# An attention and MLP block on one core: seven weight slices prepared during the first row maxima, later loads respaced, one pair of products left in its place

## The chip, the core and the metric

The kernel runs on one core of a Trainium2 chip. The core has TensorE (matrix products, into PSUM), VectorE, ScalarE and GpSimd (called POOL in the profile), which work in parallel, each on its own instructions and strictly in their order. SyncE (SP) issues all DMAs of this kernel, also in order: where a DMA's operand isn't ready, SP waits, and all DMAs behind it wait with it. The metric is the device time of one execution in microseconds. The kernel before took 1708.81 us (median of 3 runs, 1708.61 to 1709.07).

## What is computed

One transformer block with modulation (adaLN), sequence 2048, width 512, 32 heads of 16 columns, MLP width 1792, all in float32:

```
mod = silu(c) @ w_mod              # six vectors sa, ca, ga, sb, cb, gb
h = layernorm(x) * (1 + ca) + sa
x = x + ga * (softmax(q k^T / 4) v, all heads) @ wo       # q, k, v from h @ wqkv
h = layernorm(x) * (1 + cb) + sb
x = x + gb * mish(h @ w1 + b1) @ w2
```

## The kernel before

**Precision.** Operands of most products are split in a high and a low part (`hi_copy`, `lo_sub`, lines 89 and 97), and a product is made as high*high + high*low + low*high. Weights are split once by the kernel itself and put into scratch in DRAM: 14 slices of w1, 4 of wo, 14 of w2, each 128x512, called preps here. wo and w2 are multiplied by a gate before the split; w1 is not. `prep_unit` (line 656) loads a raw slice (256 KB), splits it on POOL five half-steps later and puts both halves back (512 KB) nine or more half-steps after the load.

**Groups and steps.** The 2048 rows are cut in 4 blocks of 512, the heads in 8 groups of four, so there are 32 groups n of 16 steps t each. A step works on two things at once. It makes scores of its own group, 128 keys by 512 queries for four heads (`score`, products on line 531), with exponentials on ScalarE into tiles `p0` to `p3` (3 or 4 buffers each), and two steps later the products with the values (`pv`, line 549). And it makes row maxima of scores for the group whose scores come 20 steps later (`max_tile`, product on line 482, maximum on VectorE on line 484). When a group's maxima are complete, they are transposed (`max_rows`, line 509), split, and put as two extra rows into the group's query tile (`qa<-mt`, line 520); scores then come out with the maximum taken off. Products that use 64 rows of the array run in pairs, one on each half.

**Hooks.** Everything else is hung on half-steps: `at(h, f)` runs `f` when the program text is at half-step h = 2t or 2t+1. A hook sets the order of instructions on each engine, not a time. "Position" is h modulo 32, that is, the place in a group. Before t = 0 there are 20 steps (h = -40 to -1) that make only maxima, two double products a step (`max_pair`, line 488, products on line 496, maxima on line 498), and fill TensorE with whole units (below). The exponentials' tiles are not in use there.

**Units.** The projections of q, k and v, then for each block of rows the output projection (wo), the up products (w1) and the down products (w2), are cut in units of 6 to 12 products. In the first 20 steps `whole_units` (line 1151) runs units as they come, with the PSUM banks `ms` and `acc` in turn; later a unit's products are paired with scores and maxima in the steps (`next_part`, line 1133). When a unit is done, its `fin` empties the bank. For a unit of keys or queries this is a copy by ScalarE to `qf` (one buffer), the split by POOL into `qh` and `ql` (two buffers each), and puts to scratch (`kscr`, `qscr`) from which `load_pair` (line 316) later reads the keys and queries of two heads into `ka` and `qa` (five buffers each). In the first 20 steps the order of units is: 12 of values, 4 of keys, 1 of queries, then keys again; the fins of the four key units fall on hooks -16, -14, -10 and -8. A weight slice of q, k and v for such units is loaded by `slice_load` and split by `slice_split` (`wh` on ScalarE, `wl` on POOL).

**The early pair.** Where a unit begins in a step, the last score of the step's own half of the array and the last maximum of the other half are issued ahead of it (in `step`, line 1230). Step 2 of a group is the one in which the last products of the group before have just ended and their sums are copied out of PSUM (`ot`, line 563).

**Places in program order.** Just before the first 20 steps SP issues the constants and the copies `ka<-ka` (line 1360). At hook -40 the next slice of query weights is loaded, at hooks -22 and -8 head pairs 2 and 3, at -3 the first values. `start_preps` (line 1327) chains the preps from hook 60: `load_at` (line 193) and `store_at` (line 188) move loads and puts out of the positions around the puts of `mt` (position 26), and a load also waits for the put of the tile that it takes. The MLP opens (`prep_step`, line 1338) when both the last query unit and the last prep are through; `first_loads` (line 800) then loads what the first block needs. Scores of group n start at hook 32n, its first maxima at 32n - 40.

Of the kernel before, what the change touches and what calls it, by code (L numbers as in the profile page):

```python
# [8 lines left out]
F32 = mybir.dt.float32  # L9
F32R = mybir.dt.float32r  # L10
# [8 lines left out]
def adaln_block(ctx: ExitStack, tc: tile.TileContext, x, wqkv, wo, w1, b1, w2, c, w_mod, out):  # L19
    nc = tc.nc  # L20
    P = 128
# [4 lines left out]
    DK = D // P  # L26
    FT = F // P
    TB = 512
# [10 lines left out]
    PRO = 16 + LEAD  # L39
    CUT1, CUT2 = (0, 1), (2, 3)  # L40
    LOV = ((1,), (), (1, 3), (1, 3))
    PREP = 4
# [46 lines left out]
    def hi_copy(eng, hi, src):  # L89
        if eng == "a":  # L90
            nc.scalar.copy(hi, src)
        elif eng == "v":
            nc.vector.tensor_copy(hi, src)
        else:
            nc.gpsimd.tensor_scalar(hi, src, 1.0, 0.0, op0=ALU.mult, op1=ALU.add)

    def lo_sub(eng, lo, src, hi):
        (nc.gpsimd if eng == "p" else nc.vector).tensor_sub(lo, src, hi.bitcast(F32))  # L98
# [93 lines left out]

    def load_at(h):

        return h if h < 60 or 2 <= h % 32 < 20 else h - h % 32 + 28 if 20 <= h % 32 <= 28 else h + -(h - 2) % 32

    def at(h, f):

        hooks.setdefault(h, []).append(f)
# [98 lines left out]
    def load_q(pp, rows=50):  # L298
        n, j = divmod(pp, 2)
        qb, g = divmod(n, G)  # L300
        h = 4 * g + 2 * j
        qt = qa[pp % NR].bitcast(F32)
        assert (0, h // 8, qb) in put_away, (pp, put_away)
        for s in range(2):
            nc.sync.dma_start(qt[64 * s:64 * s + rows, :], qscr[h + s, :rows, qb * TB:(qb + 1) * TB])

    def load_k(pp, tb=None):
        n, j = divmod(pp, 2)
        h = 4 * (n % G) + 2 * j
        kt = ka[pp % NR].bitcast(F32)  # L310
        at_ = slice(0, S) if tb is None else slice(tb * TB, (tb + 1) * TB)
        assert {(1, h // 8, i) for i in (range(NB) if tb is None else (tb,))} <= put_away, (pp, put_away)
        for s in range(2):
            nc.sync.dma_start(kt[64 * s:64 * s + 48, at_], kscr[h + s, :, at_])

    def load_pair(pp):
        load_q(pp)
        load_k(pp)
# [144 lines left out]
    ap = ctx.enter_context(tc.tile_pool(name="ap", bufs=1, reuse_waits="tile"))  # L463
# [224 lines left out]
    def load_y(qb, i):  # L688
        y = mst["p"].tile([P, D], F32, tag="y", name="y", bufs=5)
        r = 4 * qb + i  # L690
        nc.sync.dma_start(y, x[r * P:(r + 1) * P, :])
        return y
# [73 lines left out]
    NA = 7  # L766
# [3 lines left out]
    def block(qb, t0):  # L770
# [3 lines left out]
        y, w1s, w2s, wos = state[qb]  # L774
# [3 lines left out]
        def load(h, d, load_, keys):  # L778

            for j, k in enumerate(keys):  # L780
                at(h + 2 * j, lambda k=k: d.__setitem__(k, load_(k)))

        def more_w2(h, n):

            for j in range(n):
                k = mst["w2 at"]
                b, i = divmod(k, DK + FT)
                mst["w2 at"] += 1
                if b < NB - 1:
                    d, f, i = (state[b][3], load_wo, i) if i < DK else (state[b][2], load_w2, i - DK)  # L790
                    load(h + 2 * j, d, f, (i,))
                    if f is load_wo and i == DK - 1:
                        mst["wo at", b] = h + 2 * j
                elif i >= DK and i < DK + 3:
                    load(h + 2 * j, state[b][2], load_w2, (i - DK,))
                else:
                    mst["w2 at"] -= 1
                    break

        def first_loads(h):  # L800
            mst["w2 at"] = 0
            more_w2(h + 1, NA)
            load(h + 2, y, lambda i: load_y(qb, i), range(4))
            load(h + 9, w1s, load_w1, range(2))
            for i in range(4):
                mst["y at", qb, i] = h + 2 + 2 * i

# [111 lines left out]
        n = len(groups)  # L919
# [21 lines left out]
        for gi in range(2):  # L941
            f = 4 * gi + 5
# [22 lines left out]
    _, w1s, w2s, wos = state[last]  # L965
# [159 lines left out]
    cur = {"left": [], "fin": None, "part": []}  # L1125
# [48 lines left out]
    def step(t):  # L1174
        second = t % 2
        n, u = t // 16, t % 16 // 2
        tm = t + PRO
        run_hooks(2 * t)
        if t < 0:

            for i in range(2):
                if tm < 16:
                    kb, jq = divmod(2 * tm + i, 8)
                else:
                    jq, kb = tm % 16 // 2, 2 * second + i
                max_pair(tm // 16, jq, kb)
            if second and tm % 16 == 15:
                neg_max(tm // 16)
            run_hooks(2 * t + 1)
            for f in ats.pop(t, []):  # L1190
                f()
            whole_units(2 * t + 1, CREDIT)
            do_specials(2 * t + 1)
            return
        s = 0 if second else 1
        own, others = ([score(n, j, v, 2 * u + i) for i in range(2) for j in range(2)] for v in (s, 1 - s))
        if not second and 1 < t < T:
            next_part(2 * t)
        part = list(cur["part"])
        f = len(part)  # L1200
        if t >= T:
            if t == T:
                cur["tag"] = "acc"
            run_hooks(2 * t + 1)
            pv(t - 2)
            whole_units(2 * t + 1, 8)
            do_specials(2 * t + 1)
            return
        if tm < T:
            o = max(0, (8 - f) // 2)  # L1210
            mo, alone = maxima(tm // 16, tm % 16 // 2, s, o)

            mine = [x for p in zip(mo, own) for x in p] + own[len(mo):]
        else:
            o = max(0, (4 - f) // 2)
            mine = own[o:] if second else own[:4 - o]
            alone = others[4 - o:] if second else others[:o]

            m = len(mine)
            if f > m:  # L1220
                mine = [mine[(i * m) // f] if (i + 1) * m // f > i * m // f else None for i in range(f)]
        beside = part + alone

        def emit(product):
            e = product()
            if e is not None and cur.pop("want", None):
                cur["after"] = e

        mid = False
        if cur.pop("new", None) and alone and len(mine) > f:  # L1230

            emit(mine.pop())
            emit(beside.pop())
        for i in range(max(len(mine), len(beside))):
            if i == len(mine) // 2:
                run_hooks(2 * t + 1)

            if not f and tm < T and i == (2 if mst.get("norming") else 3):
                pv(t - 2)
                mid = True  # L1240
            if i < f:
                last = i + 1 == f
                if i < len(mine) and mine[i] and not last:
                    emit(mine[i])
                for m in beside[i]:
                    mm_half(m, second, cur.pop("after", None))
                if last:
                    cur["want"] = True
                    if i < len(mine):
                        emit(mine[i])  # L1250
                    if second and not cur["left"]:
                        cur["fin"](2 * t + 2)
                        cur["fin"] = None
            else:
                for x in (*mine[i:i + 1], *beside[i:i + 1]):
                    emit(x)
        if tm < T and tm % 16 == 15:
            neg_max(tm // 16)
        do_specials(2 * t + 1)
        if not mid:  # L1260
            pv(t - 2)
        for f in ats.pop(t, []):
            f()
# [59 lines left out]
    preps = [(w1scr[f], w1[:, f * P:(f + 1) * P].rearrange("(k p) m -> p k m", p=P), None) for f in range(FT)]  # L1323
    preps += [(woscr[k], wo[k * P:(k + 1) * P, :], 0) for k in range(DK)]
    preps += [(w2scr[f], w2[f * P:(f + 1) * P, :], 1) for f in range(FT)]

    def start_preps(h, i=0, turn=0, puts=()):

        if i == len(preps):
            mst["open"] = (max(puts) + 2) // 2  # L1330
            return
        three = (2, 1, NKC - 1) in put_away
        prep_unit(h, three and turn % 3 == 2, *preps[i])
        puts = (*puts, store_at(h + 9))[-3 if three else -2:]
        then = load_at(max(h + PREP, puts[0] + 1 if len(puts) > 2 - (not three) else 0))
        at(then, lambda: start_preps(then, i + 1, turn + 1 if three else 0, puts))

    def prep_step(t):
# [4 lines left out]

    for n in range(NIT):
        if n > 2:
            at(32 * (n - 2) + (15 if n % 2 == 0 else 9), lambda n=n: load_pair(2 * n))
        if n > 1:
            at(32 * (n - 1), lambda n=n: load_pair(2 * n + 1))
        if n > 0:
            at(32 * n - 11, lambda n=n: load_v(n))  # L1350
    at(-3, lambda: load_v(0))
    at(17, lambda: load_pair(4))
    for qb in range(NB - 1):
        t0 = 32 * G * (qb + 1) + 16
# [15 lines left out]
    t = T + 2  # L1370
# [32 lines left out]
```

## Time and profile before

| | |
|---|---|
| median of 3 runs | 1708.81 us |
| the profiled execution | 1705.6 us |
| its span, first to last instruction | 1703.8 us |
| TensorE busy | 1675.0 us (98%) |
| VectorE, ScalarE, POOL busy | 1437.6, 1356.9, 807.6 us |
| DMA | 240.08 MB, mean 141 GB/s |

The profile shows one execution. A row of a timeline gives the start in us from the first instruction, the duration, the engine (PE is TensorE, PEld its weight loads, DVE VectorE, ACT ScalarE; SPq is an issue of a DMA by SP), the line of the kernel, the operation, output<-input by the program's names, shapes and a count of merged instructions; in brackets stands the idle time before it and what ended it. A row of the stretches gives the stretch, its length, the busy time of PE, PEld, DVE, ACT and POOL with their counts, the granted clock, the mean busy share of the 16 DMA engines, and GB/s. Ends of products are modelled, so the starts are what is read.

### The profile page before, as it was taken

Reading aid. Unit: us, or ns where it says so; the run is one execution under the profiler, and the core shown is the slowest. Engines: PE = TensorE matmul, PEld = TensorE weight load, DVE = VectorE, ACT = ScalarE, POOL = GpSimd, SP = SyncE. Lnnn points to the kernel's source line nnn. Section 1 sums busy time; section 2 is a strip of 40 time slices with the busy share of each in tenths; the row PEclk is TensorE's granted clock in tenths of the full one; section 3 lists DMA queues with packets and bytes.
Section 4 is the critical chain, followed back from the end, with each engine's and each line's share of the span. In section 5 each row is a group of like instructions: output and inputs, shape, how many; then the busy total and the mean of one; then the engine's idle time right before and its main releaser. Section 6 shows DMA issues by size and latency. Waiting matters only on the chain.

```text
span 1703.8 us, 33660 instructions
## 1 busy us (share of the span) xinstructions
PE 1675.0 (98%) x12372; PEld 915.5 (54%) x12372; DVE 1437.6 (84%) x2368; ACT 1356.9 (80%) x2613; POOL 807.6 (47%) x829
## 2 busy tenths in 40 slices
PE   7999999999999999999999999999999999999999
PEld 5755665555445455555555455555545445554587
DVE  6888888888889888888889898888889888883377
ACT  6257777777778988888888998888878988888574
POOL 5155224665413464655423564556323654555442
PEclk9999999999999999999999999999999999999999
DMA  7777457777773342434355433424354433424261
GB/s 253 187 235 214 109 162 216 237 234 222 234 208 101 99 109 76 134 80 126 83 151 148 118 74 94 139 76 126 88 143 124 124 93 83 137 68 157 84 228 63
DMA packets 113997, 240.08 MB, mean 141 GB/s; under 512 B 24048, under 2 KB 49648, under 8 KB 107784
## 3 DMA queue, kind: packets, MB, share of 16 engines
q1 hardware_dynamic: 113832, 237.92, 48.6%
q8 instruction: 98, 1.61, 0.4%
q14 instruction: 67, 0.55, 0.1%
HBM read 179.95 MB, written 51.44 MB: 136 GB/s over the span
## 4 chain that ended last, share of the span: by engine, by line
PE 84%; DMA 5%; ACT 4%; DVE 4%; issue 1%; SPq 0%; POOL 0%; ACTq 0%; DVEq 0%; POOLq 0%
PE bk L549 26%; PE ring L531 20%; PE ring L482 18%; PE bk L135 10%; PE bk L129 4%; DVE mx L484 3%; ACT pr L534 3%; PE ring L1110 2%; PE ring L129 2%; DMA qa<-mt 1%; DMA ka<-kscr 1%; PE ring L496 1%; DMA w<-woscr 1%; ACT hb L722 1%; PE ring L843 0%
## 5 line engine op out<-in xcount | busy, mean ns | idle before, releaser
L484 DVE TENSOR_REDUCE mx<-ring 128x1 f32<-128x512 f32 x1968 | 1222.0, 681 | 159.9 <-PE ring L482 142.1
L534 ACT ACTIVATE pr<-ring 128x512 f32<-128x512 f32 x2048 | 1078.2, 602 | 217.8 <-PE bk L135 128.1
L482 PE MATMUL ring<-ka,qa 64*128 64x512 f32 x1968 | 815.7, 429 | 5.2 <-ACT pr L534 3.5
L531 PE MATMUL ring<-qa,ka 64*128 64x512 f32 x2048 | 759.2, 403 | 6.5 <-DMA qa<-mt 3.7
L549 PE MATMUL bk<-pr,vg 128*32 128x512 f32 x4096 | 545.1, 604 | 0.0
L482 PEld LDWEIGHTS ring<-ka,qa 64*128 64x128 f32 x1968 | 349.1, 184 | 321.6 <-DVE mx L484 230.2
L531 PEld LDWEIGHTS ring<-qa,ka 64*128 64x128 f32 x2048 | 373.5, 184 | 200.2 <-DVE mx L484 129.8
L135 PE MATMUL bk<-h,w 64*128 64x512 f32 (+1 forms) x1080 | 279.6, 391 | 0.1
L135 PE MATMUL bk<-w,a_h 64*128 64x512 f32 x632 | 211.6, 413 | 0.3 <-ACT pr L534 0.2
L135 PEld LDWEIGHTS bk<-h,w 64*128 64x128 f32 x1080 | 178.5, 184 | 13.0 <-ACT pr L534 4.3
L549 PEld LDWEIGHTS bk<-pr,vg 128*32 128x32 f32 x4096 | 80.8, 108 | 137.7 <-issue 126.4
L135 PE MATMUL bk<-w,a_l 64*128 64x512 f32 x316 | 124.0, 392 | 0.0
L135 PEld LDWEIGHTS bk<-w,a_h 64*128 64x128 f32 x632 | 107.5, 184 | 16.9 <-ACT pr L534 8.3
L899 POOL TENSOR_TENSOR y<-yd,y 128x512 f32<-128x512 f32 x44 | 56.8, 1292 | 90.5 <-ACT yd L898 85.3
L734 POOL TENSOR_SCALAR qq<-ee 128x512 f32<-128x512 f32 x25 | 15.5, 619 | 171.5 <-ACT ee L728 171.5
L750 POOL TENSOR_TENSOR qq<-qq,rr 128x512 f32<-128x512 f32 x42 | 54.2, 1289 | 83.8 <-ACT rr L744 83.6
L736 POOL TENSOR_TENSOR hb<-hb,ee 128x512 f32<-128x512 f32 x42 | 54.1, 1287 | 82.7 <-DVE ee L732 80.7
L135 PE MATMUL bk<-w,o_hl 64*128 64x512 f32 x288 | 79.2, 404 | 0.0
L98 POOL TENSOR_TENSOR a_l<-hb,a_h 128x512 fp32r<-128x512 f32 x53 | 72.0, 1358 | 4.4
L135 PEld LDWEIGHTS bk<-w,a_l 64*128 64x128 f32 x316 | 58.3, 184 | 4.9
L135 PE MATMUL bk<-h_h,wl 64*128 64x512 f32 x168 | 57.1, 420 | 0.0
L752 POOL TENSOR_TENSOR rr<-rr,qq 128x512 f32<-128x512 f32 x42 | 54.1, 1287 | 3.5
(189 smaller groups left out, 1841.5 us busy)
## 6 DMA issues: line engine op xcount, KB each, us to landing
ka<-kscr SPq DMA_DIRECT2D x124, 384.0 KB
w<-w2scr SPq DMA_DIRECT2D x56, 512.0 KB
w<-w1scr SPq DMA_DIRECT2D x46, 512.0 KB
vg<-vscr SPq DMA_DIRECT2D x32, 552.0 KB
qa<-qscr SPq DMA_DIRECT2D x124, 100.0 KB
kscr<-qh SPq DMA_DIRECT2D x16, 512.0 KB
qscr<-qh SPq DMA_DIRECT2D x32, 256.0 KB
hl<-in_B_w SPq DMA_DIRECT2D x28, 256.0 KB
```

The costliest lines, as they stand in the source:

```text
L98: (nc.gpsimd if eng == "p" else nc.vector).tensor_sub(lo, src, hi.bitcast(F32))
L129: nc.tensor.matmul(acc, l, r, start=start, stop=stop)
L135: i = nc.tensor.matmul(acc, l[64 * g:64 * g + 64], r[64 * g:64 * g + 64], start=start and not g, stop=bool(stop and g))
L482: nc.tensor.matmul(pm, qt[64 * s:64 * s + 64, qs * P:(qs + 1) * P], kt[64 * s:64 * s + 64, kb * TB:(kb + 1) * TB], start=True, stop=True)
L484: nc.vector.tensor_reduce(out=mxs[n][:, s, 4 * j + qs, kb:kb + 1], in_=pm, op=ALU.max, axis=AX.X)
L531: nc.tensor.matmul(p_, kt[64 * s:64 * s + 64, kc * P:(kc + 1) * P], qt[64 * s:64 * s + 64, :], start=True, stop=True)
L534: e = nc.scalar.activation(pr, p_, AF.Exp, scale=SCALE)
L549: nc.tensor.matmul(accs[n][32 * h:32 * h + 32, :], vgs[n][:, o:o + 32], pts.pop((t, h)), start=(kc == 0), stop=(kc == 15))
L736: (nc.vector if tail else nc.gpsimd).tensor_mul(hb, hb, ee)
L750: nc.gpsimd.tensor_mul(qq, qq, rr)
L752: nc.gpsimd.tensor_mul(rr, rr, qq)
L899: nc.gpsimd.tensor_add(y[i], yd, y[i])
```

## The change

Seven of the 14 slices of w1 are loaded at hooks -40, -37, ... -22, split five half-steps later on POOL and put back eight after the load, in tiles `p1` and `p3`; `start_preps` begins with the eighth. `load_at` keeps loads of slices out of positions 0 to 3 (before: 0 and 1), and a load keeps two half-steps behind the put of its tile instead of one. The even head pair of a group from 3 on is loaded at position 2 (group 6: 15 as before) instead of 15 or 9. `first_loads` (called at the MLP's opening) loads the four slices of wo at once, and no longer with them three of w2 and two of w1; these five follow at hooks 279 to 287. The early pair is left in its place in step 2 of a group.

```diff
     def load_at(h):
-        return h if h < 60 or 2 <= h % 32 < 20 else h - h % 32 + 28 if 20 <= h % 32 <= 28 else h + -(h - 2) % 32
+        return h if h < 60 or 4 <= h % 32 < 20 else h - h % 32 + 28 if 20 <= h % 32 <= 28 else h + -(h - 4) % 32
...
         def first_loads(h):
             mst["w2 at"] = 0
-            more_w2(h + 1, NA)
+            more_w2(h + 1, DK)
             load(h + 2, y, lambda i: load_y(qb, i), range(4))
-            load(h + 9, w1s, load_w1, range(2))
+            load(t0 + 7, w1s, load_w1, range(2))
+            at(t0 + 10, lambda: more_w2(t0 + 11, NA - DK))
...
-        if cur.pop("new", None) and alone and len(mine) > f:
+        if cur.pop("new", None) and alone and len(mine) > f and t % 16 != 2:
...
-    def start_preps(h, i=0, turn=0, puts=()):
+    EARLY = 7
+
+    def early_prep(i, h):
+
+        scr, src, _ = preps[i]
+        lo, hi = [ap.tile([P, TB], F32R, tag=f"p{1 + i % 2 * 2}", name="ep", bufs=4) for _ in range(2)]
+        raw = lo.bitcast(F32)
+        nc.sync.dma_start(raw.rearrange("p (k m) -> p k m", m=P), src)
+
+        def split():
+            hi_copy("p", hi, raw)
+            lo_sub("p", lo, raw, hi)
+
+        def put():
+            for v, part in enumerate((hi, lo)):
+                nc.sync.dma_start(scr[:, v, :], part.bitcast(F32))
+
+        at(h + 5, split)
+        at(h + 8, put)
+
+    for i in range(EARLY):
+        at(3 * i - 2 * PRO, lambda i=i: early_prep(i, 3 * i - 2 * PRO))
+
+    def start_preps(h, i=EARLY, turn=0, puts=()):
...
-        then = load_at(max(h + PREP, puts[0] + 1 if len(puts) > 2 - (not three) else 0))
+        then = load_at(max(h + PREP, puts[0] + 2 if len(puts) > 2 - (not three) else 0))
...
-            at(32 * (n - 2) + (15 if n % 2 == 0 else 9), lambda n=n: load_pair(2 * n))
+            at(32 * (n - 2) + (15 if n == 6 else 2), lambda n=n: load_pair(2 * n))
```

## The prediction

> **What bounds the kernel now.** I read the page's totals first, then the chain of waits, then the timelines of the engines around the places that the change touches.
>
> ```profile
> span 1703.8 us, 33660 instructions
> PE 1675.0 (98%) x12372; PEld 915.5 (54%) x12372; DVE 1437.6 (84%) x2368; ACT 1356.9 (80%) x2613; POOL 807.6 (47%) x829
> ...
> PE 84%; DMA 5%; ACT 4%; DVE 4%; issue 1%; SPq 0%; POOL 0%; ACTq 0%; DVEq 0%; POOLq 0%
> ```
>
> TensorE sets the end. A step of attention ends with the eight products of probabilities with values (line 549), so their starts count the steps. A step without any wait, in the second MLP block:
>
> ```profile
> 1095.29 1.06 PE L549 MATMUL bk<-pr,vg 128*32 128x512 f32 x8
> ...
> 1098.13 1.07 PE L549 MATMUL bk<-pr,vg 128*32 128x512 f32 x8
> ```
>
> That is 2.84 us. The number of products is fixed and the change removes none, so it can win only where steps are longer, and lose only where it makes a step wait. Four of the long steps wait for a DMA:
>
> ```profile
> 339.87 0.47 PE L531 MATMUL ring<-qa,ka 64*128 64x512 f32 x1 [1.37 <-DMA qa<-mt]
> ...
> 386.84 0.47 PE L531 MATMUL ring<-qa,ka 64*128 64x512 f32 x1 [0.87 <-DMA qa<-mt]
> ...
> 434.38 0.46 PE L531 MATMUL ring<-qa,ka 64*128 64x512 f32 x1 [1.42 <-DMA qa<-mt]
> ...
> 491.77 0.46 PE L482 MATMUL ring<-ka,qa 64*128 64x512 f32 x1 [0.68 <-DMA od<-ot]
> ```
>
> The first three, 3.66 us together, are the first scores of groups 4, 5 and 6 (step 80, 96, 112), which need the row maxima (`mt`) in their query tile. The fourth, in step 132, is put down to `od<-ot`, but a maximum reads only `qa` and `ka`: it is the load of head pair 19, asked for at hook 256 and read at 264.
>
> **Part 1: no early pair in step 2 of a group.** In the step in which the sums of the group before leave PSUM (copy `ot`), ScalarE also empties the finished unit (`hb`), and the early pair puts a score first:
>
> ```profile
> 674.27 1.06 PE L549 MATMUL bk<-pr,vg 128*32 128x512 f32 x8
> 674.67 0.68 ACT L722 ACTIVATE hb<-bk,b1c 128x512 f32<-128x512 f32 x1
> ...
> 675.72 0.60 ACT L563 COPY ot<-bk 128x512 f32<-128x512 f32 x1
> ...
> 676.18 2.10 ACT L534 ACTIVATE pr<-ring 128x512 f32<-128x512 f32 x4
> ...
> 676.87 0.50 PE L482 MATMUL ring<-ka,qa 64*128 64x512 f32 x1 [0.17 <-ACT pr L534]
> ...
> 677.21 0.39 PE L531 MATMUL ring<-qa,ka 64*128 64x512 f32 x1
> ...
> 677.54 1.06 PE L549 MATMUL bk<-pr,vg 128*32 128x512 f32 x8
> ```
>
> The step takes 677.54 - 674.27 = 3.27 us, 0.43 more than 2.84. The ring has six banks, so the seventh product of the step takes the bank of the first, here the early score, whose exponential ends at about 676.87. Without the early pair the first product is a maximum and the first score the second one; the bank waited for is then wanted by the eighth product, the last. That one starts at 676.87 instead of 677.21: 0.34 us saved. What the early pair covered is the unit's bank, free when `hb` ends at 675.35, against 675.27 for TensorE's arrival (674.27 and the 1.00 us of eight products): 0.1 us, inside the wait that remains. A unit begins in such a step at 18 hooks (h = 36, 68, 260; 324 to 548 and 772 to 964 by 32). In 13 of them the step has this pattern, as here in step 482 (3.24 us):
>
> ```profile
> 1516.17 1.06 PE L549 MATMUL bk<-pr,vg 128*32 128x512 f32 x8
> ...
> 1519.41 1.06 PE L549 MATMUL bk<-pr,vg 128*32 128x512 f32 x8
> ```
>
> Of the other five, in two (548, 804) the unit before ends in a VectorE addition and the pair covers its wait, which I cost at nothing either way; three (36, 68, 868) show no such excess. 13 x 0.34 = **-4.4 us** (ends: -6 if all 18 give it, -2 if the unit's bank wait eats half).
>
> **Part 2: respaced slices and loads.** Why `mt` was late shows on SP, which issues all DMAs in order:
>
> ```profile
> 319.39 0.50 SPq L667 DMA_DIRECT2D w1scr<-hl  x1
> 326.72 0.33 SPq L660 DMA_DIRECT2D hl<-in_A_wo  x1
> ...
> 328.35 0.38 SPq L469 DMA_DIRECT2D vg<-vscr  x1
> 328.82 2.13 SPq L264 DMA_DIRECT2D qscr<-qh  x2
> ...
> 332.20 4.74 SPq L520 DMA_DIRECT2D qa<-mt  x4
> ```
>
> SP stands still from 319.9 to 326.7, because the raw slice goes into a tile whose put was issued at 319.39. Everything behind it bunches: a put, 552 KB of values and 768 KB of queries enter the queues just ahead of `mt`, whose four issues stretch to 4.74 us. I worked out the new hooks from the recurrence in `start_preps`: with 25 slices left, loads fall at positions 28, 4, 8, 12, 16 of each 32 half-steps and puts at 5, 13, 17, 21, 2 (before: loads at 28, 2, 6, 10, 14, 18). Only the load at 16 still stands three half-steps behind its tile's put (13); before, two in each group did (14 and 18), and the second started late because of the first. So SP should be on time at 21, and the bulk drains five half-steps (7 us) before `mt` at 26. I take the three waits as gone: **-3.7 us** (ends -3.7 and 0, since put, values and queries now all sit at 21). The pair loads move to position 2, right behind the other pair's at 0, which is the more urgent and stays ahead; no wait of TensorE hangs on them. At the opening of the MLP three w2 slices and two w1 slices no longer stand ahead of pair 19: **-0.7 us** (ends -0.9 and 0). MLP weights at hooks 279 to 287 are read from 300 on. The opening itself moves from step 121 to 120 only, since the last query unit (hook 237) bounds it; the second halves of the projection still wait for hook 276, so no unit moves to fill more steps.
>
> **Part 3: seven slices among the first maxima.** These are seven loads (256 KB), seven splits on POOL, fourteen puts (256 KB each), in program order at hooks -40 to -14. What stands around them:
>
> ```profile
> 70.65 3.83 SPq L1360 DMA_DIRECT2D ka<-ka  x6
> 74.53 0.65 SPq L226 DMA_DIRECT2D wr<-in_A_wqkv  x1
> ...
> 76.65 2.43 SPq L305 DMA_DIRECT2D qa<-qscr  x2
> ...
> 81.97 0.83 SPq L268 DMA_DIRECT2D kscr<-qh  x1
> ```
>
> ```profile
> 78.90 0.62 ACT L91 CAST wh<-wr 128x512 fp32r<-128x512 f32 x1 [2.37 <-DMA wr<-in_A_wqkv]
> ...
> 79.60 1.29 POOL L98 TENSOR_TENSOR wl<-wr,wh 128x512 fp32r<-128x512 f32 x1 [26.80 <-ACT wh L91]
> 81.31 0.63 POOL L95 TENSOR_SCALAR qh<-qf 128x512 fp32r<-128x512 f32 x1 [0.42 <-ACT qf L254]
> 82.02 1.29 POOL L98 TENSOR_TENSOR ql<-qf,qh 128x512 fp32r<-128x512 f32 x1
> ...
> 91.58 0.62 POOL L95 TENSOR_SCALAR qh<-qf 128x512 fp32r<-128x512 f32 x1 [4.61 <-DMA kscr<-qh]
> ...
> 93.77 0.59 ACT L254 COPY qf<-bk 128x512 f32<-128x512 f32 x1 [4.40 <-POOL ql L98]
> ```
>
> ```profile
> 50.18 0.73 PE L496 MATMUL ring<-ka,qa 64*128 64x512 f32 x4
> ...
> 88.50 1.09 PE L129 MATMUL bk<-h_h,wh 128*128 128x512 f32 x4
> ```
>
> ```profile
> 187.23 0.45 SPq L660 DMA_DIRECT2D hl<-in_B_w  x1
> ...
> 190.31 0.62 POOL L95 TENSOR_SCALAR hl<-hl 128x512 fp32r<-128x512 f32 x1 [9.27 <-DMA hl<-in_B_w]
> 191.01 1.29 POOL L98 TENSOR_TENSOR hl<-hl 128x512 fp32r<-128x512 f32 x1
> ```
>
> TensorE reaches hook -40 at 50.18, but SP gets to that hook's DMA only at 74.53: it is 24 us behind. So POOL's idle 26.80 us are not to be had: the first early load leaves at 75.2. POOL works in order too, and all seven splits (hooks -35 to -17) come ahead of its work on the first key unit (81.31; hook -16). From there the cover is gone step by step: `qf` has one buffer, so ScalarE's copy of the second key unit waits for `ql` of the first (the 4.40 us at 93.77 is that same wait); that copy frees the bank which the fourth key unit takes, at 88.50, and TensorE stops there.
>
> The floor goes by POOL alone: load in 75.2 + 3.1 (187.23 to 190.31) = 78.3; seven splits of 1.99 (190.31 to 192.30) = 92.2; the slice's `wl` 1.3, the first unit 2.0, ScalarE's copy 0.6: 96.1, against 88.50: **+7.6**.
>
> The likelier cost has the DMAs in it. Slice 4 takes slice 0's tiles and slice 6 slice 2's, so each load waits on SP for a put to land, and the next put stands behind that load. The same stretch shows 4.4 us for a load (74.53 to 78.90) and up to 9.6 for a put (81.97 to 91.58).
>
> ```profile
> 75.00:100.00 25.00, 24.78 (x116) 15.74 (x115) 22.84 (x23) 4.60 (x9) 10.22 (x11) 1.00 1.01 280
> ```
>
> With 4.4 and, for puts half as large as that key put, 6: load 0 in at 79.6, split 81.6, put landed 87.7, load 4 and put 2 behind it, landed 94.4, load 6 in at 98.9, split 100.9, first key unit 102.9, copy 103.5: +15. By bytes: seven loads, the puts of four slices ahead of the last, two value puts (544 KB each) and the query slice are 5.3 MB, 19.0 us at the 280 GB/s of the row: last load in at 94.2, its split, the first unit and the copy 4.6: 98.8, +10. The second count lets no DMA engine idle while SP waits for a put, so I take **+13.5**, nearer to the chain; with puts of 9.6 the chain gives +22. Nothing later returns it: the steps behind are paced by TensorE.
>
> The Trainium skill ("DMA: Bandwidth & Descriptors", section Anatomy of one DMA) gives about 2 us fixed plus the bytes at 436 GB/s, an estimate of 2.6 us for each of these transfers; by it POOL's chain binds and the cost is about +7. The row says 4.4 and 9.6 there, with the DMA engines full, so I go by the row.
>
> **Sum.** -4.4 - 3.7 - 0.7 + 13.5 = +4.7 us. The profiled execution took 1705.6 us (span 1703.8 and 1.8 around it), 3.2 below the runs' median 1708.8; added to that, **1713.5 us**.
>
> **Rivals.** (a) Faster: SP reaches the early loads as TensorE does, POOL does them in its idle 26.80 us before 79.60, and part 3 costs nothing: -8.8, 1700.0. It decides if the first load leaves before about 62 us (seven splits, 14 us, and a load of 3.1 then end before 79.60). Against it: the order of SP's instructions ahead of it is untouched. (b) Only POOL's floor binds: -1.2, 1707.6. (c) The long puts of 81.97 hold for the early slices, +22, and half of parts 1 and 2 comes: +17.6, 1726.4. (d) The respacing does not do what it says: put, values and queries, all at position 21, still stand in front of `mt`: 3.7 more, 1717.2.
>
> **How the numbers follow.** A measurement of this kernel tells about 0.2% (3.4 us) from no change. Forecast 0.40, (a) 0.18, (b) 0.15, (c) 0.14, (d) 0.13. Time 1713.5. Range 1703 to 1726: it holds the forecast's own range (1710 to 1715, from 10 and 15 us), (b) and (d) and reaches to (c), leaving (a) and what lies beyond (c). Slower is (c), (d) and most of the forecast, 0.62; same is (b) and the forecast's low end, 0.18; faster 0.20.
>
> **What would show it.** First early load at about 75 us; POOL's first `qh` at 95 to 101 instead of 81.31; a wait of TensorE of 8 to 15 us at the fourth key unit, put down to ScalarE's copy; first scores of step 0 later by as much; steps 80, 96 and 112 at 2.9 us; steps like the one at 674.27 near 2.9. The forecast is wrong if the first step of attention starts no later than before, or if the 3.27 us steps stay.

## The result and the profile after

| | before | after |
|---|---|---|
| median (lowest to highest), 4 runs each | 1708.71 us (1707.56 to 1709.07) | 1728.07 us (1726.04 to 1728.47) |
| the profiled execution, its span | 1705.6, 1703.8 us | 1727.78, 1726.0 us |

The ratio is 1.0119, with a 95% interval of 1.0105 to 1.0132: the changed kernel is 19.4 us slower, where +4.7 was forecast. The totals of its profile:

```profile
span 1726.0 us, 33682 instructions
...
PE 1681.4 (97%) x12372; PEld 926.1 (54%) x12372; DVE 1439.0 (83%) x2368; ACT 1358.6 (79%) x2613; POOL 808.5 (47%) x829
```

The counts on all engines are those of before, since the same work was only moved. TensorE's busy time grew by 6.4 us, the span by 22.2; most of the loss is standing still. Where it lies is read by counting steps again: the start of the products of line 549 of each step, set against the same step of before.

| from before's execution, at the products of step | 2 | 258 | 274 | 386 | 402 | last |
|---|---|---|---|---|---|---|
| after | +18.8 | +12.3 | +19.3 | +19.6 | +23.3 | +22.2 |

So 18.8 us are lost before the first step, some 7 are won over the rest, and 10.7 are lost at two places, each a few steps behind the start of a new block of rows (steps 261, 262 and 389, 390).

**Before the first step.** The timelines of SP, POOL, ScalarE and TensorE around the first key units:

```profile
75.71 2.11 SPq L1335 DMA_DIRECT2D ep<-in_B_w  x3
...
97.46 4.55 SPq L1343 DMA_DIRECT2D w1scr<-ep  x4
102.14 0.37 SPq L268 DMA_DIRECT2D kscr<-qh  x1
```

```profile
97.75 1.26 POOL L98 TENSOR_TENSOR ep<-ep 128x512 fp32r<-128x512 f32 x1
98.98 0.62 POOL L95 TENSOR_SCALAR qh<-qf 128x512 fp32r<-128x512 f32 x1
...
108.97 0.62 POOL L95 TENSOR_SCALAR qh<-qf 128x512 fp32r<-128x512 f32 x1 [5.34 <-DMA kscr<-qh]
111.03 1.28 POOL L98 TENSOR_TENSOR ql<-qf,qh 128x512 fp32r<-128x512 f32 x1 [1.44 <-DMA kscr<-ql]
```

```profile
100.98 0.59 ACT L254 COPY qf<-bk 128x512 f32<-128x512 f32 x1 [19.66 <-POOL ql L98]
...
112.34 0.59 ACT L254 COPY qf<-bk 128x512 f32<-128x512 f32 x1 [8.10 <-POOL ql L98]
```

```profile
101.61 2.07 PE L129 MATMUL bk<-h_h,wh 128*128 128x512 f32 x4 [12.86 <-ACT qf L254]
...
114.03 0.50 PE L496 MATMUL ring<-ka,qa 64*128 64x512 f32 x2 [1.66 <-DVE mt L514]
...
115.17 0.50 PE L496 MATMUL ring<-ka,qa 64*128 64x512 f32 x2 [0.64 <-DVE mx L498]
...
121.21 0.47 PE L531 MATMUL ring<-qa,ka 64*128 64x512 f32 x1 [0.80 <-DMA qa<-mt]
```

The last early split ends POOL's run at 99.0, its first key unit follows at 98.98, ScalarE's copy of the second unit has waited 19.66 us for it, and TensorE starts the fourth key unit at 101.61 instead of 88.50: 13.1 us. The rest of the 18.5 us by which the first score is late (121.21 against 102.67) lies, on TensorE's own timeline, behind that wait: 3.1 us in the three shorter waits shown, and 2.3 us at half the clock. The stretches of the same trace show the latter:

```profile
104.00:106.00 2.00, 2.00 (x7) 0.74 (x5) 0.26 (x1) 0.25 (x1) 0.00 (x0) 0.50 1.06 393
106.00:108.00 2.00, 2.00 (x9) 1.63 (x8) 2.00 (x2) 0.00 (x0) 0.00 (x0) 0.79 1.05 407
108.00:110.00 2.00, 2.00 (x12) 1.14 (x11) 1.41 (x4) 0.00 (x0) 0.62 (x1) 1.00 1.06 398
```

The granted clock (third number from the end) is 0.50 until past 106. The first twelve products behind the wait (eight of the unit, four of the maxima) take 5.03 us (to 106.64) instead of 2.71.

What TensorE waits for first need not be what makes the first score late. POOL's third key unit is late by as much: its `ql`, at 111.03 above, stood at 92.44 in the kernel before, 18.6 us earlier. Which of the two set the loss is taken up under part 3 below. The rows of the kernel before, POOL's and the first score:

```profile
92.44 1.29 POOL L98 TENSOR_TENSOR ql<-qf,qh 128x512 fp32r<-128x512 f32 x1 [0.25 <-DMA kscr<-ql]
```

```profile
102.67 0.50 PE L531 MATMUL ring<-qa,ka 64*128 64x512 f32 x1
```

**At the block boundaries.** SP, VectorE and TensorE of the changed kernel around step 261:

```profile
871.66 0.76 SPq L305 DMA_DIRECT2D qa<-qscr  x2
872.47 0.89 SPq L314 DMA_DIRECT2D ka<-kscr  x2
874.91 0.34 SPq L673 DMA_DIRECT2D w<-w2scr  x1
877.25 0.36 SPq L904 DMA_DIRECT2D out<-y  x1
877.75 0.61 SPq L574 DMA_DIRECT2D sm<-ot  x1
```

```profile
887.71 0.25 DVE L584 RECIPROCAL rc<-sm 128x16 f32<-128x16 f32 x1 [5.85 <-DMA sm<-ot]
```

```profile
880.65 1.07 PE L549 MATMUL bk<-pr,vg 128*32 128x512 f32 x8
...
888.56 0.79 PE L531 MATMUL ring<-qa,ka 64*128 64x512 f32 x1 [5.26 <-DVE mx L484]
...
889.28 1.94 PE L549 MATMUL bk<-pr,vg 128*32 128x512 f32 x8
```

And in the kernel before, SP and VectorE at the same step:

```profile
862.22 0.61 SPq L574 DMA_DIRECT2D sm<-ot  x1
...
873.23 0.69 SPq L305 DMA_DIRECT2D qa<-qscr  x2
```

```profile
869.45 0.24 DVE L584 RECIPROCAL rc<-sm 128x16 f32<-128x16 f32 x1
```

`sm` holds the sums of the group that has just ended (8 KB), and VectorE's reciprocal reads it. Before, the even pair's load was issued 11 us behind it, and the reciprocal started without a wait. Now the pair stands ahead of it as well, beside the odd pair, weights and rows of the residual that stood there before too. `sm` is issued 3.2 us later relative to the steps (15.5 us after its counterpart, where the steps are 12.3 behind), and lands 9.9 us after its issue. VectorE, in order, stops 5.85 us with the maxima behind it, and TensorE runs out of banks. The step takes 8.63 us (880.65 to 889.28).

### The profile page after: what moved, and what is told of

Read it like the earlier page. It is cut to its first block, busy times and chain, and to the rows that moved or that the text cites. A ratio compares the mean times of both kernels' runs of the same rounds, so it can differ in the third digit from the quotient of the medians.

```text
span 1726.0 us, 33682 instructions
## 1 busy us (share of the span) xinstructions
PE 1681.4 (97%) x12372; PEld 926.1 (54%) x12372; DVE 1439.0 (83%) x2368; ACT 1358.6 (79%) x2613; POOL 808.5 (47%) x829
## 4 chain that ended last, share of the span: by engine, by line
PE 87%; DMA 5%; DVE 3%; ACT 3%; SPq 1%; issue 1%; POOL 0%; ACTq 0%; POOLq 0%; DVEq 0%
PE bk L549 28%; PE ring L531 21%; PE ring L482 19%; PE bk L135 10%; PE ring L129 3%; PE ring L1111 2%; DVE mx L484 2%; ACT pr L534 2%; PE bk L129 1%; DMA sm<-ot 1%; DMA w1scr<-ep 1%; DMA kscr<-ql 1%; DMA xt<-in_A_x 1%; DMA qa<-mt 1%; DMA w<-woscr 1%
## 5 line engine op out<-in xcount | busy, mean ns | idle before, releaser
L135 PEld LDWEIGHTS bk<-w,a_h 64*128 64x128 f32 x632 | 106.9, 184 | 15.9 <-ACT pr L534 8.3
L498 DVE TENSOR_REDUCE mx<-ring 128x2 f32<-128x1024 f32 x40 | 46.8, 1218 | 19.5 <-PE ring L496 19.5
L95 POOL TENSOR_SCALAR qh<-qf 128x512 fp32r<-128x512 f32 x27 | 16.8, 621 | 88.7 <-ACT qf L254 53.6
```

What stands on the lines that cost most here:

```text
L135: i = nc.tensor.matmul(acc, l[64 * g:64 * g + 64], r[64 * g:64 * g + 64], start=start and not g, stop=bool(stop and g))
L498: nc.vector.tensor_reduce(out=mxs[n][:, :, jq, kb:kb + 1], in_=pm, op=ALU.max, axis=AX.X)
```

## The experiments

In each batch the times are set against runs of the kernel before on the same chip: 1707.72 us (17 runs) for the first four, 1708.23 us (21 runs) for the last three.

**1. The head pairs back where they were.** The changed kernel with one line undone:

```diff
-            at(32 * (n - 2) + (15 if n == 6 else 2), lambda n=n: load_pair(2 * n))
+            at(32 * (n - 2) + (15 if n % 2 == 0 else 9), lambda n=n: load_pair(2 * n))
```

> The changed kernel with the even head pairs loaded at positions 15 and 9 again, as before the change; all else as changed. Theory (pair loads): in the changed kernel two reciprocals on VectorE, in steps 261 and 389, wait 5.85 and 2.62 us for the sums (sm<-ot), whose DMA stands behind two head pairs asked for at positions 0 and 2; with the even pair back behind the sums these waits go, the steps 261, 262, 389 and 390 (8.63, 4.03, 5.11, 4.33 us) fall to about 2.9 each, and the time falls by 10.5 us from 1728.1 to about 1717.5. The waits for mt in steps 80 and 112 stay gone, since those hang on the slices. Rival (weights): the wo, w2 and y loads of the MLP at the block boundary delay the sums, and the pair is only one of several: the four steps stay above 3.5 us and the time at 1724 or more. Rival (mt): the pair at position 15 is what bunched SP in front of mt; then the waits of 1.4 us in steps 80 and 112 come back and the time is about 1721.

Measured: 1718.96 us (1717.41 to 1720.22), ratio 1.0065 [1.0052, 1.0078], 9.1 us less than after. The long steps are gone; the products of steps 260 to 262 start at

```profile
883.10 1.06 PE L549 MATMUL bk<-pr,vg 128*32 128x512 f32 x8
...
886.01 1.07 PE L549 MATMUL bk<-pr,vg 128*32 128x512 f32 x8
...
888.85 1.06 PE L549 MATMUL bk<-pr,vg 128*32 128x512 f32 x8
```

and `sm`, in SP's and VectorE's timelines, is read 7.1 us after its issue without a wait:

```profile
877.24 0.62 SPq L574 DMA_DIRECT2D sm<-ot  x1
```

```profile
884.31 0.25 DVE L584 RECIPROCAL rc<-sm 128x16 f32<-128x16 f32 x1
```

Steps 261, 262, 389 and 390 take 2.91, 2.84, 2.90 and 2.84 us, the shift stays at +14.8 to +15.2 from step 258 to 402, steps 80 and 112 stay at 2.84 and 2.85, and step 96 takes 3.57 instead of 3.25. So the pair at position 2 made the boundary stalls and had no part in the gain at `mt` of steps 80 and 112. In the profiled execution the first step starts at +20.5 instead of +18.8, so the last step is 8.1 us earlier and not 10.7.

**2. The pair rule alone.** The kernel before with the one condition:

```diff
-        if cur.pop("new", None) and alone and len(mine) > f:
+        if cur.pop("new", None) and alone and len(mine) > f and t % 16 != 2:
```

> The kernel before with the early pair left in its place in step 2 of a group, and nothing else changed. Theory (bank of the early score): about 13 steps of 3.2 to 3.3 us fall; by the prediction's 0.34 us each the time is 1708.7 - 4.4 = 1704.3; by the 0.24 us that the same steps show in the changed kernel (3.26 to 3.02) it is 3.1 to 3.7 less, about 1705.3. Rival: the pair covers as much of the unit's bank wait as it costs, the steps stay at 3.2 and the time within 1 us of before.

Measured: 1704.22 us (12 runs, 1702.15 to 1709.15), ratio 0.9983 [0.9973, 0.9993], and in the trace -3.0 us from the first step to the last. The step that was quoted at 3.27 us:

```profile
674.47 1.06 PE L549 MATMUL bk<-pr,vg 128*32 128x512 f32 x8
...
677.09 0.47 PE L482 MATMUL ring<-ka,qa 64*128 64x512 f32 x1
677.49 1.07 PE L549 MATMUL bk<-pr,vg 128*32 128x512 f32 x8
```

It takes 3.02 us: the gain is real, 0.24 us a step.

**3. The early slices alone.** The kernel before with `early_prep`, its seven hooks and `start_preps` from the eighth slice on; spacing, pairs, MLP weights and the pair rule as before.

```diff
+    for i in range(EARLY):
+        at(3 * i - 2 * PRO, lambda i=i: early_prep(i, 3 * i - 2 * PRO))
...
-    def start_preps(h, i=0, turn=0, puts=()):
+    def start_preps(h, i=EARLY, turn=0, puts=()):
```

> The kernel before with the seven early slices (loads, splits, puts at hooks -40 to -14) and the later chain starting at the eighth; pair loads, spacing, MLP loads and the early pair as before. Theory (POOL's order and SP's lateness): the first score starts at about 121 us instead of 102.7, 18.5 us later, with a wait of TensorE near 13 us at the fourth key unit and a granted clock of 0.50 behind it; the waits for mt in steps 80, 96 and 112 stay at 0.9 to 1.4 us, since the remaining slices keep their spacing; time 1708.7 + 18.5 = 1727. Rival (fewer slices are what clears mt): the three waits go although the spacing is as before, and the time is about 1723. Rival (pairs): part of the 18.5 us comes from the other edits, and the time is below 1722.

Measured: 1724.62 us (1720.97 to 1725.78), ratio 1.0094 [1.0078, 1.0110]. The first step starts at +19.1 and the last at +18.3: all of the loss is in the prologue, and nothing returns it. TensorE's wait at the fourth key unit is 10.34 us here, 2.5 shorter than in the changed kernel, and still the first step is no earlier. The boundary steps are as before. Steps 80 and 96 keep their waits (4.49 and 4.56 us), step 112 loses its own (2.95), which had been put down to the spacing.

**4. The early slices without POOL's part.** The changed kernel with the 14 splitting instructions left out; the raw slice is put for both halves, so that seven slices of w1 are not split and what they feed is not the reference's.

```diff
         def split():
-            hi_copy("p", hi, raw)
-            lo_sub("p", lo, raw, hi)
+            pass
...
-            for v, part in enumerate((hi, lo)):
+            for v, part in enumerate((lo, lo)):
```

> The changed kernel without the fourteen POOL instructions that split the seven early slices; the raw slice is put back for both halves, so the seven slices of w1 in the products are not the reference's; loads and puts stay. Theory (POOL): POOL's work on the first key unit starts near 81 us again, the wait of 12.9 us at the fourth key unit goes, and only SP's lateness is left: head pair 2, asked for at 92.6 us in the changed kernel and read in step -4 (92.9 before), makes TensorE wait 2 to 6 us; first score at 105 to 109 us, time 1728.1 - 12 to 16 = 1712 to 1716. Rival (DMA): the seven loads and fourteen puts on SP and on the DMA engines hold up the key units' puts and the pair by as much; the first score stays at 117 us or later and the time above 1723.

Measured: 1726.37 us (1723.37 to 1732.58), ratio 1.0113 [1.0094, 1.0132], hardly less than after; the first step starts at +15.9. POOL's and SP's timelines:

```profile
81.78 0.63 POOL L95 TENSOR_SCALAR qh<-qf 128x512 fp32r<-128x512 f32 x1 [1.89 <-ACT qf L254]
82.50 1.29 POOL L98 TENSOR_TENSOR ql<-qf,qh 128x512 fp32r<-128x512 f32 x1
...
106.98 0.62 POOL L95 TENSOR_SCALAR qh<-qf 128x512 fp32r<-128x512 f32 x1 [19.54 <-DMA kscr<-qh]
```

```profile
95.03 3.76 SPq L1342 DMA_DIRECT2D w1scr<-ep  x4
99.21 0.37 SPq L268 DMA_DIRECT2D kscr<-qh  x1
```

POOL does the first key unit at 81.78, as before the change, and the stall at the fourth key unit is gone; TensorE waits later instead, for head pair 2 and for `mt`:

```profile
97.88 0.52 PE L496 MATMUL ring<-ka,qa 64*128 64x512 f32 x1 [4.42 <-DMA ka<-kscr]
...
110.77 0.79 PE L496 MATMUL ring<-ka,qa 64*128 64x512 f32 x2 [5.50 <-DVE mt L514]
```

The put of the first key unit, ready at 83.8, is issued only at 99.21, behind the early loads and puts in SP's order, and POOL's third key unit waits 19.54 us until it has landed. The theory that POOL's splits are the cost thus fell, and its rival held: without them the first step is only 2.9 us earlier, and the other 15.9 hang on the loads and puts in SP's order.

**5. SP less behind.** The changed kernel with DMAs that stood in SP's order just ahead of the first maxima (the zero rows for `qa` and the constants) moved into the loop over the four 512-row parts ahead of it:

```diff
+            if tb == 2:
+                for i in range(2, NR):
+                    zeros(i)
+            if tb == 3:
+                constants()
...
-            for i in range(2, NR):
-                zeros(i)
...
-        constants()
```

> The changed kernel with the constants' DMAs (rows of zeros for three query tiles, the scratch's zeros, the MLP's bias) issued among the loads of the first keys, where SP stands waiting at 48 to 52 and 55 to 58 us, instead of behind them; all else as changed. Theory (SP is 24 us late at hook -40): SP reaches the first early load some 7 to 10 us earlier than 75.7, all that hangs on it (the splits, head pair 2, the key units' puts) moves with it, the wait of TensorE at the fourth key unit falls from 12.9 us to 3 to 6, and the first score comes at 110 to 114 instead of 121.2: time 1728.1 - 7 to 10 = 1718 to 1721. Rival (bandwidth): the DMA engines, full from 75 to 115 us in the changed kernel, set the pace and the earlier start only moves data into a stretch that is as full; the first score moves by less than 3 us.

Measured: 1724.38 us (1723.51 to 1725.54), ratio 1.0088 [1.0070, 1.0106]. SP's and TensorE's timelines:

```profile
70.86 1.66 SPq L1337 DMA_DIRECT2D ep<-in_B_w  x3
```

```profile
98.01 2.08 PE L129 MATMUL bk<-h_h,wh 128*128 128x512 f32 x4 [8.77 <-ACT qf L254]
...
117.15 0.50 PE L533 MATMUL ring<-qa,ka 64*128 64x512 f32 x1
```

The first early load leaves 4.85 us earlier than after, the wait at the fourth key unit is 4.09 shorter and the first score 4.06 earlier. (Line numbers are two higher in this kernel.) An earlier start of SP's chain thus reaches the first score almost whole, more than the 3 us that the bandwidth rival allowed. The time missed the expected 1718 to 1721 because SP gained less than the 7 to 10 us expected.

**6 and 7. No early slices, and two.** The changed kernel with the pairs as in experiment 1, `EARLY = 0` and the loads of slices from position 2, as before; the two half-steps behind a put, the later MLP weights and the pair rule stay; and the same with `EARLY = 2` and SP's order of experiment 5.

```diff
-    EARLY = 7
+    EARLY = 0
```

> The changed kernel without early slices (all 32 in the later chain), with the loads of slices allowed at positions 2 and 3 and the even pairs at 15 and 9 as before; the two half-steps behind a put, the MLP loads moved to 279 to 287, and the early pair's rule stay. Theory (sum of parts): no wait ahead of step 0 (first score at 102.7), the rule's 3 to 3.5 us as measured by itself, 0.7 to 0.9 from step 132, and of the three waits for mt those that the spacing alone clears: 1704 if none, 1701 if all. Rival: the later opening (step 123 instead of 121) leaves steps without units and costs 2 us or more; time 1706 or above.

> As the kernel without early slices, but with two slices early and the constants' DMAs issued among the loads of the first keys. Theory (POOL and SP both have room for two when SP comes 7 to 10 us earlier): two splits end on POOL before its work on the first key unit, which comes at 81 to 83 us, TensorE does not wait at the fourth key unit, first score at 102.7 to 104; with 30 slices in the chain the opening is at step 120 and the time is the other kernel's, give or take 1 us. Rival (any early slice costs): its puts stand ahead of head pair 2 and the key units' puts, the first score comes at 107 or later and the time is 4 us or more above the kernel without.

Measured: without early slices 1704.45 us (10 runs, 1700.17 to 1708.84), ratio 0.9969 [0.9956, 0.9982]; with two 1705.57 us (12 runs, 1703.40 to 1709.79), ratio 0.9983 [0.9972, 0.9995]. Both beat both kernels; the first has the lowest ratio measured here, not told apart from experiment 2 (their intervals overlap). With two slices the first score starts 2.3 us later than before, at 104.98, between what was expected and its rival. The waits for `mt` did not go with the two half-steps alone. In the trace without early slices:

```profile
385.66 0.46 PE L531 MATMUL ring<-qa,ka 64*128 64x512 f32 x1 [0.74 <-DMA qa<-mt]
...
434.10 0.46 PE L531 MATMUL ring<-qa,ka 64*128 64x512 f32 x1 [2.10 <-DMA qa<-mt]
```

Steps 80, 96 and 112 take 2.84, 3.63 and 5.23 us there, and 7.36, 2.85 and 3.17 with two slices: the wait moves between the groups.

## Why the prediction was right or wrong

| term | forecast | measured in the trace of after |
|---|---|---|
| early slices, to the first step | +13.5 | +18.8 |
| pair rule | -4.4 | -3.0 (what the next two rows leave of -7.3) |
| waits for `mt`, steps 80, 96, 112 | -3.7 | -3.4 (12.32 us to 8.94) |
| step 132 | -0.7 | -0.9 |
| pair loads at position 2 | 0 | +10.7 |
| sum | +4.7 | +22.2 |

**The step that failed** is the sentence of part 2 that the pair loads stand "right behind the other pair's at 0, which is the more urgent and stays ahead; no wait of TensorE hangs on them". It asked who reads the pair, and when, but not what is queued behind it. Behind it comes `sm<-ot`, 8 KB, which VectorE's in-order reciprocal needs. Where a block begins the cover is gone: 6.9 us at steps 261 and 262, 3.7 at 389 and 390 (each against 5.73 before). Experiment 1 shows it, by taking only this away. At other groups the same move cost nothing visible. The kernel itself says why these places are tight: for the last group of a block (`hurry` in `evac`) the reciprocal hangs 8 instead of 12 half-steps behind. In the kernel before it started 7.2 and 6.8 us after the issue of `sm` at the two places, and 13.6 us or more after it at most other groups. At the first block boundary it came as early in the changed kernel (7.8 us) without a wait; there only the pairs stood just ahead of `sm`, where the other two have weights and residual rows too. That these are needed for the stall is argued from this, not tried. Which counts more in the lateness of `sm`, the 3.2 us of SP's delay or the longer landing, was not tried separately.

**Part 3** was right in most of its links, wrong in the one that closes the chain, and 5.3 us short. The first early load left at 75.71 (said: 75.2), POOL's first `qh` came at 98.98 (95 to 101), the fourth key unit waited 12.86 us (8 to 15) for ScalarE's copy and started 13.1 us late (13.5). The sum ended there and took the stretch from the fourth key unit to the first score as unchanged. That stretch grew by 5.4: half the clock behind the stall (2.3) and the waits of 1.66, 0.64 and 0.80. But the chain of waits of the changed kernel, which is followed back from the end, does not pass the 12.86 us wait. It runs from the early loads and puts on SP to the put of the first key unit, which lands 8.13 us after its issue and on which POOL's third key unit waits, then by ScalarE's fourth copy to `mt`, for which TensorE waits again at 114.03:

```profile
75.71 4.73 DMA ep<-in_B_w
...
84.14 4.32 DMA w1scr<-ep
...
89.58 5.48 DMA w1scr<-ep
...
95.12 7.57 DMA w1scr<-ep
...
102.75 8.13 DMA kscr<-ql
```

The runs tell the two apart. Set against the kernel before, in us:

| run | wait at the fourth key unit | POOL's `ql` of the third key unit, later by | first step, later by |
|---|---|---|---|
| after | 12.86 | 18.6 | 18.8 |
| experiment 1 | 12.89 | 19.9 | 20.5 |
| experiment 3 | 10.34 | 18.0 | 19.1 |
| experiment 4 | none | 15.4 | 15.9 |
| experiment 5 | 8.77 | 13.9 | 14.5 |
| two slices | none | 2.2 | 2.3 |

The first step follows POOL's third key unit within 1.1 us, and not the wait. So the sum left out the put of the first key unit behind the early slices; that the stall it did forecast came so near (13.1 for 13.5) says little about the loss, and what the stall and the slow clock behind it cost by themselves was not shown. As for the rivals: (a) fell, since SP was late as read. (b), POOL alone with +7.6, fell, and with it the sum by the Trainium skill ("DMA: Bandwidth & Descriptors", section Anatomy of one DMA); its estimate of 2.6 us for one of these transfers stands against 4.32 to 7.57 for the early puts in the chain above. That section fits DMAs issued by GpSimd, and this kernel's are issued by SP. (c) came near the total, 1726.4, but not by its own way: the early slices cost 18.8 and not 22, and the gains were not halved. "Nothing later returns it" held: experiment 3 ends at +18.3 from +19.1.

**Part 1** was right in direction and place, and 0.1 us a step too high. The last product did start at the time said, 2.62 us into the step (677.09 - 674.47; said 2.60). But the next step follows it by 0.40 us (677.49 - 677.09), where the prediction took over the 0.33 of the row at 677.21: a step of 3.02 and not of 2.93. 13 x 0.24 = 3.1, and experiment 2 shows 3.0.

**Part 2's waits for `mt`** came out near the sum, but not for the reason given. Steps 80 and 112 lost theirs, 96 kept 0.36 of waiting. With early slices alone step 112 is clear and 80 and 96 are not; with the two half-steps behind a put and no early slices 80 is clear and 112 is worse. All edits together, which also leave fewer slices for the groups, clear most. Which transfer makes the wait in each group was not settled, so rival (d) is neither confirmed nor excluded. The drop of step 132 to 2.84 us came as said, but it came in experiment 3 as well, without the deferred MLP weights, so its cause stays open.

## What to carry to other kernels

Ask of a load that is moved earlier not only who reads it, but which small transfer now stands behind it in the same queue, and which in-order engine waits for that; 8 KB behind a head pair cost more here (10.7 us) than the rest of the change won (7.3). An engine's idle time is only to be had if its work can reach it: read how far the issuing engine is behind the program order at that place (here 24 us) before filling the gap. And where a stall is forecast, follow the other late outputs as well, up to the place where the chains meet: here a put that stood behind the new transfers set the first score, and not the stall that was foreseen.

## What the hardware showed that was not expected

The mean granted clock of the kernel before was 1.000; here, behind the 12.86 us stall it was 0.50 for some 5 us of running products (101.61 to about 106.8, from the 0.79 of the stretch 106 to 108). The Trainium skill ("TensorE: Matmul & The Clock Gate", section Part 1: The HAM clock gate) says that TensorE's clock halves after at least one idle window of about 3.4 us and returns after at least one busy window of that length. The halving agrees. The return took 5.2 us here; behind the 5.26 us wait of step 261 the clock was 0.50 from 888.5 to about 891.9, 3.3 us from the first product.

The 8 KB of `sm` landed late behind the pair. The chain of waits of the changed kernel has `sm<-ot` twice:

```profile
877.75 9.93 DMA sm<-ot
...
1257.06 8.13 DMA sm<-ot
```

In experiment 1 and before, at the first of these places, it was in use 7.1 and 7.2 us after its issue, with no wait for it.
